# A fused attention and gated feed-forward kernel: new prices, new waits and new due times in the plan that sets the order of its instructions

## The chip, the cores and the metric

The kernel runs on one core of a Trainium2 chip. A core has several engines, each with its own in-order queue: TensorE (PE in the profile; its weight loads are shown apart as PEld), VectorE (DVE), ScalarE (ACT), GpSimd (POOL), and SyncE (SP), which here issues all DMA transfers. Engines wait for each other by semaphores. The metric is the device time of one execution in microseconds, the median of several runs.

## The reference

Eight batches of eight-head attention over 576 positions with head size 64, then a two-layer feed-forward with a gate. Cut to what matters:

```python
scores = np.matmul(q, k.transpose(0, 1, 3, 2)) / np.sqrt(D)        # (8, 8, 576, 576)
scores = np.where(block_i >= block_j, scores, -1e9)                # blocks of 64 positions
attn = np.exp(scores - scores.max(-1, keepdims=True))
attn = attn / (attn.sum(-1, keepdims=True) + 1e-9)
x = (attn @ v).transpose(0, 2, 1, 3).reshape(4608, 512)
h = x @ w_in                                                       # (512, 2048)
g = h * np.tanh(np.log1p(np.exp(np.minimum(h, 20))))               # mish
out = g @ w_out                                                    # (2048, 512)
```

All inputs and the output are float32.

## The kernel before

**Precision.** TensorE's large products use float16. Each operand is scaled by a power of two and split into a high half (a cast) and a low half (the remainder), and a product is the sum of three: high by high, high by low, low by high. The split is made by a cast on ScalarE, VectorE or GpSimd, and a subtraction on VectorE (`p_hi`, `p_lo`, lines 1088 to 1106, for the exponentials; `xh`, `xl`, lines 834 to 849, for queries and keys; `xt_hi`, `xt_lo`, lines 1211 to 1221, for the attention's output; `Gt`, lines 1350 to 1365, for the gated values). The heads of batch 0 alone are computed by float32 products (lines 954 and 1125), since nothing is split yet when the kernel begins.

**Attention.** A batch's 576 query positions are cut into two halves of 384 and 192. For each pair of heads (`load_pair`), each head and each half (`attend`), the work is a chain:
- first pass of scores on TensorE into a PSUM buffer `ss` (line 940, or 954 for batch 0); there are two such buffers;
- the maximum over key blocks, by copies (line 1003, ScalarE or VectorE) and `tensor_max` on VectorE (line 1016) into `mt`; these read PSUM;
- the maximum over partitions on GpSimd, `partition_all_reduce` into `mr` (line 1045);
- the negated maximum written into a row of `QB` (line 1052 on VectorE or 1059 on ScalarE);
- a second pass of scores that adds this row (line 940);
- the exponential on ScalarE (line 1070), a masking memset on GpSimd (line 1081), the split into `p_hi` and `p_lo`;
- the value products into the PSUM buffer `u` (line 1125), the sums and the division (lines 1172 to 1198), the split into `xt_hi` and `xt_lo`.

**Feed-forward.** Each half batch is a `Tile`, 16 in all. `turn` transposes its rows by DMA into `x_hi` and `x_lo` (line 1259). `m1` makes the products with `w_in` (line 1292) in four groups of 512 of the 2048 hidden columns and applies mish on ScalarE (line 1318) into `Et`, which has five slots, one for a group. `split` makes `Gt` from `Et`. `m2` makes the products with `w_out` (line 1394), scales them (line 1426 or 1433) and stores them.

**Shared space.** `Et` also holds batch 0's queries, keys and values in float32 until its heads are done, laid out pair by pair over the five slots. `Gt` holds pieces of `w_out` while the weights are read as 64-bit words and put together by integer operations on VectorE (lines 538 and 555), so the first `split` waits for all of `w_out`.

**The order.** No order is written by hand. Every step is an operation in a `Plan`: an engine with a price in microseconds, or several engines that could do it; the operations that it waits for; buffers taken and freed. `Plan.go` (line 164) plays the plan through engine by engine, taking at each engine the ready operation with the earliest due time. `Plan.order` (line 257) does so from the due times in the table `DUE`, passed back along the waits, then six times more backward and forward again, and keeps the shortest. The instructions are then emitted in the order of their planned starts, which fixes each engine's queue and which engine does a step that several could do. On the chip, semaphores wait for the true ends; the plan's times only set the order. The prices are small functions, which before read:

```python
def products(ns, full=False, rows=128):        # line 292; full: float32
    if full:
        return sum(n / 600 + 0.004 for n in ns), sum(n * rows / 32 for n in ns)

def pool(n):                                   # line 307
    return 0.42 + n / 300

def elem(n):                                   # line 311, casts on GpSimd
    return 0.2 + n / 780
```

The plan also models TensorE's clock (`pe_end`, line 239), table loads on ScalarE and transfers in flight.

Of the kernel before, what the change touches and what calls it, by code (L numbers as in the profile page):

```python
# [30 lines left out]
    "w": ((-17, 129.5, 276.5, 98), (186, 152, 293, 88)),  # L31
    "batch": (104, 216.5, 449.5, 454.5, 299.5, 543.5, 719.5, 647.5),
    "load": (
        (154.5, 254, 279, 266.5),
        (60, -40.5, 297, -132),
        (207.5, 299, 178.5, 157),
        (187, 199, 325, 217),
        (290, 323.5, 527.5, 588.5),
        (306.5, 436.5, 792, 494),
        (453.5, 894, 760.5, 651),  # L40
        (594.5, 471, 795.5, 666),
        (765, 662.5, 663.5, 727),
    ),
    "tile": (
        (-30.5, 39, -33.5, 25.5, 197.5, 303.5, 50, 51.5,
         254.5, 136.5, 239, 372, 191.5, 89, 162,
         278.5, 250.5, 219, 277.5, 192, 294.5, 190.5),
        (185.5, 251.5, -2.5, 309.5, 130.5, 233, -1, 73,
         102.5, 121.5, 148, 239, 158, -40.5, 279,
         358, 211.5, 275, 339, -89, 270.5, 268),  # L50
        (118.5, 386, 335.5, 400.5, 461.5, 282.5, 238, 182.5,
         418, 308.5, 219.5, 365, 379.5, -73.5, 297,
         314, 287.5, 305, 304, 380.5, 466.5, 271),
        (136, 112.5, 125, 241, 322.5, 144, 214, 393.5,
         459, 297, 395, 376, 444, -0.5, 291.5,
         307, 543, 524.5, 351, 337.5, 467.5, 195),
        (231, 326, 363, 300.5, 551.5, 477.5, 275.5, 335,
         336, 367.5, 368.5, 557, 415, -15, 587,
         624, 374, 360.5, 403, 630.5, 404, 785),
        (409.5, 381, 272.5, 532, 541.5, 549.5, 302, 496,  # L60
         404.5, 325, 449, 612.5, 457.5, 15, 441.5,
         417.5, 463, 526, 710, 290, 513.5, 304),
        (466.5, 602.5, 497.5, 373, 362.5, 311, 337, 301.5,
         502.5, 405.5, 522, 569, 411, 47, 512,
         576.5, 661, 564.5, 887.5, 719, 623.5, 582.5),
        (553, 697.5, 813.5, 516, 599, 519, 436, 516,
         568.5, 437.5, 558, 485.5, 428.5, -113.5, 511,
         568.5, 440.5, 560, 489, 239.5, 875, -158.5),
        (645, 444.5, 500.5, 908, 610, 755, 634, 470,
         563.5, 715.5, 637.5, 708, 506.5, 167.5, 666.5,  # L70
         677.5, 493.5, 637.5, 649.5, 675.5, 683, 743.5),
        (642.5, 302.5, 430, 330.5, 630.5, 547, 641.5, 619.5,
         890.5, 818.5, 558, 788, 609.5, -67.5, 753,
         610.5, 580.5, 585.5, 786.5, 53.5, 706.5, -90.5),
        (761.5, 414, 489.5, 582.5, 650, 594, 584.5, 847.5,
         865.5, 706, 756, 691, 832, -6, 825,
         700, 1028, 1041, 847, 955, 765.5, 735.5),
        (544, 643.5, 740, 539.5, 935, 669, 658, 939.5,
         799.5, 606, 745, 610, 742.5, -24.5, 878,
         698.5, 830, 882, 1243.5, 37, 892, 174),  # L80
        (804.5, 803.5, 895.5, 622, 731.5, 688.5, 716.5, 688,
         841, 726, 1131, 858, 1085, 161.5, 746.5,
         739.5, 705, 704, 923.5, 1136.5, 995.5, 777),
        (775, 681.5, 1052, 986, 790, 1115.5, 902.5, 1146,
         1028, 1017, 997.5, 1056, 1086, 98, 890,
         1003, 764.5, 1045.5, 892.5, -29.5, 962, 41.5),
        (971, 622.5, 587.5, 994.5, 1051, 814, 711, 1039,
# [35 lines left out]
class Plan:  # L123
# [16 lines left out]
    def __init__(self):  # L140
        self.ops = []

        self.slack = 0.0
# [1415 lines left out]
```

## Time and profile before

| | us |
|---|---|
| median of 3 runs (lowest, highest) | 1068.46 (1068.0, 1071.4) |
| profiled execution | 1066.92 |
| its span, first to last instruction | 1065.1 |
| PE busy in the span | 1002.3 (94%) |
| VectorE busy | 687.3 (65%) |
| ScalarE busy | 689.7 (65%) |
| GpSimd busy | 362.0 (34%) |

The granted TensorE clock has a mean of 0.97. In the profile's rows an operation reads: line, engine, operation, output tile <- input tiles, shape, count, busy time, mean time of one in ns, idle time of its engine before it and what ended it. In a timeline a row reads: start, duration, engine, line, operation, and in brackets the idle time before it with its releaser. In the rows of stretches each engine has its busy time and number of instructions; the last three numbers are the granted TensorE clock, the busy share of the DMA engines and GB/s. In rows of waits stand who waited, for whom, total us, how often, and the longest.

### The profile page before, as it was taken

The page shows a single profiled execution, that of the slowest core. Times are in us where ns is not written, and L with a number is a line of the kernel's source. Part 1 is how long each engine was busy: PE and PEld are TensorE (multiplying, and loading weights), DVE is VectorE, ACT ScalarE, POOL GpSimd, SP SyncE. Part 2 cuts the span into 40 slices and gives each one's busy share as a digit, 9 for nine tenths or more (in the row PEclk, how much of TensorE's full clock was granted, in tenths as well). Part 3 has the DMA queues.
Part 4 walks back from the last instruction along what each step waited for, and adds up shares of the span by engine and source line. Part 5 has one row for each costly group of instructions (what it writes and reads, how often), then busy time and mean ns, then how long its engine had stood idle before and what let it go on. Part 6 is the DMA issues. An engine that isn't in the chain of part 4 may idle for free. (4 is left out here: it accounts for less than half of the span.)

```text
span 1065.1 us, 25078 instructions
## 1 busy us (share of the span) xinstructions
PE 1002.3 (94%) x10016; PEld 759.3 (71%) x10016; DVE 687.3 (65%) x1520; ACT 689.7 (65%) x1047; POOL 362.0 (34%) x466
## 2 busy tenths in 40 slices
PE   4886989999999999989999999999999999999998
PEld 3564767686577777757777677876686677777777
DVE  5877799886678789777675886577771247212510
ACT  3556798658677899758875786687782466333531
POOL 3424245352544445353542642445520004000200
PEclk7668999999999999999999999999999999999999
DMA  9563432455134414443433342413441201200010
GB/s 321 185 186 100 130 101 76 117 124 145 41 109 114 126 45 129 102 116 89 124 79 80 100 127 71 118 51 89 116 87 38 59 23 44 53 9 9 16 31 24
DMA packets 118711, 98.65 MB, mean 93 GB/s; under 512 B 48449, under 2 KB 104769, under 8 KB 118593
## 3 DMA queue, kind: packets, MB, share of 16 engines
q1 hardware_dynamic: 118592, 97.04, 33.5%
q8 instruction: 79, 1.29, 0.5%
q14 instruction: 40, 0.32, 0.1%
HBM read 53.35 MB, written 9.44 MB: 59 GB/s over the span
## 5 line engine op out<-in xcount | busy, mean ns | idle before, releaser
L1394 PE MATMUL acc<-Gt,wo_h 128*128 128x192 f16 (+1 forms) x2048 | 393.2, 287 | 0.8 <-DVE ot L1426 0.8
L1045 POOL PARTITION_ALL_REDUCE mr<-mt x128 | 205.5, 1624 | 306.6 <-DVE mt L1016 290.6
L1292 PE MATMUL acc<-x_hi,wi_h 128*128 128x192 f16 (+1 forms) x1024 | 294.7, 288 | 2.3 <-ACT Et L1318 1.6
L1292 PE MATMUL acc<-x_hi,wi_l 128*128 128x192 f16 (+1 forms) x1024 | 294.6, 288 | 0.0
L1292 PE MATMUL acc<-x_lo,wi_h 128*128 128x192 f16 (+1 forms) x1024 | 294.6, 288 | 0.0
L1394 PE MATMUL acc<-Gt,wo_l 128*128 128x192 f16 (+1 forms) x1024 | 293.6, 287 | 0.0
L1292 PEld LDWEIGHTS <-wi_h 128*128 128x128 f16 x2048 | 190.0, 98 | 61.9 <-issue 7.1
L1394 PEld LDWEIGHTS <-wo_h 128*128 128x128 f16 x2048 | 190.2, 98 | 61.1 <-issue 2.1
L1318 ACT ACTIVATE Et<-acc,bv 128x384 f32<-128x384 f32 x192 | 110.0, 579 | 92.7 <-PE acc L1292 91.4
L1365 DVE SCALAR_TENSOR_TENSOR Gt<-Et,bv,Gt 128x1536 f16<-128x1536 f32 (+1 forms) x64 | 92.5, 1446 | 86.5 <-ACT Gt L1350 85.9
L1016 DVE TENSOR_TENSOR mt<-mt,ss 128x192 f32<-128x192 f32 (+3 forms) x448 | 121.5, 297 | 33.9 <-ACT mt L1003 29.4
L1106 DVE TENSOR_TENSOR p_lo<-pe,p_hi 128x896 f16<-128x896 f32 (+1 forms) x112 | 118.4, 1060 | 16.2 <-ACT p_hi L1088 11.3
L1292 PEld LDWEIGHTS <-wi_l 128*128 128x128 f16 x1024 | 100.5, 98 | 34.2 <-issue 1.5
L1394 PEld LDWEIGHTS <-wo_l 128*128 128x128 f16 x1024 | 100.3, 98 | 33.4 <-issue 0.3
L1070 ACT ACTIVATE pe<-ss,pv 128x896 f32<-128x896 f32 (+1 forms) x112 | 104.8, 953 | 21.2 <-DVE p_lo L1106 10.0
L1081 POOL MEMSET pe<- 64x64 f32 (+1 forms) x192 | 34.0, 207 | 221.6 <-ACT pe L1070 214.9
L940 PE MATMUL ss<-QB,KB 65*128 65x192 f16 (+7 forms) x512 | 68.2, 256 | 34.3 <-ACT QB L1059 22.9
L1125 PEld LDWEIGHTS <-p_hi 128*128 128x128 f16 x1680 | 86.8, 97 | 13.1 <-DVE tt L1198 2.7
L1125 PE MATMUL u<-V,p_hi 128*128 128x65 f16 (+1 forms) x1680 | 91.7, 193 | 3.1 <-DVE tt L1198 3.0
L1070 ACT ACT_TABLE_LOAD x66 | 84.7, 1283 | 14.6 <-PE ss L940 5.1
L1125 PE MATMUL u<-V,p_lo 128*128 128x65 f16 x840 | 87.3, 193 | 0.7 <-DVE p_lo L1106 0.7
L1318 ACT ACT_TABLE_LOAD x67 | 86.0, 1283 | 1.2
(105 smaller groups left out, 1205.6 us busy)
## 6 DMA issues: line engine op xcount, KB each, us to landing
QK<-xh SPq DMA_DIRECT2D x168, 72.0 KB, 2.1
out_dram<-ot SPq DMA_DIRECT2D x48, 192.0 KB, 2.0
wo_l<-in_w_in_dram SPq DMA_DIRECT2D x8, 1024.0 KB, 6.5
Gt<-in_w_out_dram SPq DMA_DIRECT2D x16, 512.0 KB, 4.2
ql<-in_q_dram SPq DMA_DIRECT2D x28, 288.0 KB, 3.2
kl<-in_k_dram SPq DMA_DIRECT2D x28, 288.0 KB, 3.2
VL<-in_v_dram SPq DMA_DIRECT2D x28, 288.0 KB, 3.1
VL<-in_v_dram SPq DMA_DIRECT2D x28, 256.0 KB, 3.2
```

The source lines that it names most:

```text
L940: nc.tensor.matmul(ss[:, col : col + q1 - qs], lhsT=k_[:, a, c * P : (c + 1) * P], rhs=q_[:, a, qs:q1], start=x == 0 and col % 512 == 0, s ...
L1016: nc.vector.tensor_max(t, t, sv(ss_[A.slot % NSS]))
L1045: lambda: nc.gpsimd.partition_all_reduce(mr[rm][:, 0:n], mx[:, 0:n], P, RED.max),
L1070: lambda: nc.scalar.activation(*spread(pe[rm], ss_[A.slot % NSS]), AF.Exp, scale=st.get("esc", D ** -0.5)),
L1081: nc.gpsimd.memset(t.rearrange("p (x y) -> p x y", x=k)[:, :, 0:64], 0.0)
L1106: lambda: nc.vector.tensor_sub(p_lo[rm][:, 0:W], pe[rm][:, 0:W], p_hi[rm][:, 0:W]),
L1125: nc.tensor.matmul(o, lhsT=l, rhs=r, start=start, stop=stop, skip_group_check=True)
L1292: nc.tensor.matmul(pt, lhsT=w[:, d, f * P : (f + 1) * P], rhs=x[:, d, :], start=k == 0 and d == 0 and z == 0, stop=d == NP - 1 and z == 2, ...
L1318: nc.scalar.activation(Et[:, (self.i * NG + g) % NE, j : j + K, 0:n], acc_[c.slot % NACC][:, 0 : K * n].rearrange("p (k n) -> p k n", k=K) ...
L1365: lambda g_hi=g_hi, g_lo=g_lo, ev=ev: nc.vector.scalar_tensor_tensor(out=g_lo, in0=ev, scalar=self.s_g, in1=g_hi, op0=ALU.mult, op1=ALU.su ...
L1394: nc.tensor.matmul(pt, lhsT=w[:, f, o * P : (o + 1) * P], rhs=g, start=k == 0 and f == 0 and z == 0, stop=f == NF - 1 and z == 2, skip_gro ...
```

## The change

Five things change, all of them in the plan; the computation stays.

- **VectorE holds GpSimd.** Operations that touch PSUM get the mark `psum=True`. While a VectorE operation without this mark runs, a GpSimd operation is planned to lose 0.82 of the overlap (`SHARE`), whichever begins first; its planned end is moved on accordingly. VectorE's own times aren't changed by GpSimd.
- **Prices.** A float32 product of at most 65 columns costs 0.226 us instead of n/600 + 0.004; a reduction on GpSimd costs 0.345 + n/356 instead of 0.42 + n/300.
- **Waits in `Et`.** The first five groups of `m1` and their mish wait for the heads of batch 0 whose inputs lie under their slot. The plan had no such wait before.
- **Tile 1 apart from tile 0.** The first `m1` product and the first mish of tile 1 (batch 0's second half) no longer wait for the last of tile 0, so that the groups of the two halves may alternate.
- **Due times.** All of `DUE` is replaced.

```diff
 DUE = {
-    "w": ((-17, 129.5, 276.5, 98), (186, 152, 293, 88)),
+    "w": ((384, 371.5, 301, 306.5), (72.5, 455, 389.5, 417.5)),
...
+    SHARE = 0.82
...
+                if done == 1 and end[i] > now:
+                    heapq.heappush(events, (end[i], 1, i))
+                    continue
...
+                if e == "dve" and not back and not ops[i].psum:
+                    locked = until[e]
+                    if until["pool"] > now:
+                        until["pool"] += self.lost(until["pool"] - now, us)
+                        end[pooled] = until["pool"]
+                if e == "pool" and not back:
+                    until[e] += self.lost(us, locked - now)
+                    pooled = i
...
+    def lost(self, us, lock):
+
+        return min(us / (1 - self.SHARE), max(lock, 0.0)) * self.SHARE
...
     if full:
-        return sum(n / 600 + 0.004 for n in ns), sum(n * rows / 32 for n in ns)
+        us = sum(n / 600 + 0.004 if n > 65 else 0.226 for n in ns)
+        return us, sum(n * rows / 32 for n in ns)
...
 def pool(n):
-    return 0.42 + n / 300
+    return 0.345 + n / 356
...
-                old.append(tiles[k // NG].splits[k % NG] if k >= 0 else [])
+                if k >= 0:
+                    old.append(tiles[k // NG].splits[k % NG])
+                    continue
+
+                w0 = (k + NE) * FG * Q0
+                old.append([
+                    x
+                    for p in range(NP)
+                    if p * FW < w0 + FG * Q0 and w0 < (p + 1) * FW
+                    for x in own[p]["ends"]
+                ])
...
                         if f == 0 and begin:
-                            after = after + [last.get("m1")]
+                            if self.i != 1:
+                                after = after + [last.get("m1")]
...
+                before = last.get("mish") if self.i != 1 else None
...
-                        [chain, self.batch["fc1"][g], last.get("mish")] + old[g],
+                        [chain, self.batch["fc1"][g], before] + old[g],
```

The mark `psum=True` is given to the copies and `tensor_max` of the maxima (lines 1003 and 1016), the sums and the division (lines 1172 to 1198) and the scaling of the outputs (line 1426).

More of the change, by code (lines that the diff above doesn't have):

```diff
@@ L149, in part, with add @@
             self.due = self.due[i]
-    def add(self, eng, us, emit, after=(), take=(), free=(), other=(), table=None):
+    def add(self, eng, us, emit, after=(), take=(), free=(), other=(), table=None, psum=False):
         self.ops.append(Op(eng, us, emit, after, take, free, self.due, other))
+        self.ops[-1].psum = psum
         self.ops[-1].table = table
@@ L1201, in attend @@
         o = add(
[L1202 removed]
+            "dve",
+            0.2 + dve(nqc * P, True),
+            weigh,
+            [sm],
+            free=[(u_ring, st["u", half][0])],
+            psum=True,
         )
```

124 lines of the change are left out of this document (63 added, 61 removed).

## The prediction

> **What bounds the kernel now.** I read the page's first part, then stretches of the span, then what the matmul engine waited for, then the places of the longest waits in order of time.
>
> ```profile
> span 1065.1 us, 25078 instructions
> PE 1002.3 (94%) x10016; PEld 759.3 (71%) x10016; DVE 687.3 (65%) x1520; ACT 689.7 (65%) x1047; POOL 362.0 (34%) x466
> ```
>
> ```profile
> core 0: us, PE busy (x) PEld busy (x) DVE busy (x) ACT busy (x) POOL busy (x), PEclk, DMA share, GB/s
> 0.00:100.00 100.00, 70.26 (x361) 49.53 (x362) 70.45 (x166) 50.58 (x90) 36.42 (x54) 0.73 0.66 205
> 150.00:800.00 650.00, 624.81 (x6889) 480.77 (x6888) 495.22 (x1118) 490.64 (x756) 284.85 (x355) 0.99 0.38 98
> 800.00:1065.10 265.10, 259.68 (x2406) 196.08 (x2404) 78.85 (x140) 106.31 (x149) 24.16 (x35) 1.00 0.11 30
> ```
>
> TensorE (PE) sets the time. The edit removes no matmul, so it can move only PE's idle time and slow clock. Idle is 1065.1 − 1002.3 = 62.8 us: 29.7 in the first 100 us, 25.2 between 150 and 800, 5.4 after that. In the first 100 us the granted clock is 0.73, so its 70.26 us of work would take about 51 at full clock: another 19 us, as an estimate. Some 80 us in all can move.
>
> PE's waits in the first 100 us, then from 100 to 850:
>
> ```profile
> PE ss L940 <- ACT QB L1059: 15.1, 3, 8.3
> PE ss L940 <- DVE QB L1052: 6.6, 4, 2.8
> ```
>
> ```profile
> PE ss L940 <- ACT QB L1059: 7.8, 5, 2.6
> PE ss L940 <- ACT pe L1070: 7.7, 12, 1.8
> PE ss L940 <- DVE QB L1052: 4.5, 7, 1.4
> ...
> PE acc L1292 <- ACT Et L1318: 1.6, 2, 1.4
> ```
>
> Most of it is the second pass of scores (L940) waiting for the negated maxima in QB, which wait for GpSimd's reduction over partitions (mr, L1045). Its longest case, from the timelines of five engines and two stretches:
>
> ```profile
> 79.70 3.48 DVE L555 SCALAR_TENSOR_TENSOR wo_h<-wo_l,wo_h 128x1024 int32<-128x1024 int32 x3
> ...
> 83.78 2.48 DVE L555 SCALAR_TENSOR_TENSOR Gt<-Gt 128x512 int32<-128x512 int32 x4
> ```
>
> ```profile
> 60.37 0.41 POOL L574 PARTITION_ALL_REDUCE wv<-wv  x1 [2.00 <-ACT wi_h L566]
> ...
> 80.84 5.74 POOL L697 PARTITION_ALL_REDUCE bv<-bv  x1 [5.98 <-ACT VL L690]
> ```
>
> ```profile
> 77.72 1.26 SPq L1259 DMA_TRANSPOSE x_lo<-xt_lo  x1
> ```
>
> ```profile
> x_lo<-xt_lo SPq DMA_TRANSPOSE x40, 2.5
> ```
>
> ```profile
> 87.88 0.85 PE L940 MATMUL ss<-QB,KB 1*128 1x192 f16 x5 [8.26 <-ACT QB L1059]
> 88.66 0.50 PE L1292 MATMUL acc<-x_hi,wi_h 128*128 128x384 f16 x1
> ```
>
> ```profile
> 80.00:90.00 10.00, 2.12 (x10) 0.97 (x10) 6.26 (x9) 2.55 (x7) 7.62 (x4) 0.65 0.54 163
> 90.00:100.00 10.00, 10.00 (x75) 7.46 (x74) 7.33 (x25) 7.92 (x10) 1.04 (x4) 0.84 0.19 49
> ```
>
> A reduction of four columns, done elsewhere in 0.41 us, lasts 5.74 while VectorE runs seven two-input integer operations for w_out, which nothing needs yet. The maxima's reduction is queued behind it on GpSimd, QB behind that, and PE stands 8.26 us. The products of w_in (L1292) stand behind the waiting L940 in PE's queue, though their last input was sent at 77.72 and takes 2.5 to land: ready at 80.2, begun at 88.66. Afterwards the clock is 0.84 for 10 us, 1.6 us more.
>
> **The change part by part.** Hardly an instruction is added or removed (copies and casts may change engine); the order is made anew by a plan with other prices, waits and due times. So the cost lies in which waits of PE go and which come.
>
> *(a) VectorE holding GpSimd, at the stop above.* A plan that charges 0.82 of the overlap sees the 5.3 us (5.74 − 0.41) that the old plan could not, and can put the integer work or the reduction of bv elsewhere. Bounds: 0, and 8.26 + 1.6 = 9.9 gained. I take 5, about the middle, because the products brought forward meet the new waits of (d).
>
> *(b) The other early reductions.*
>
> ```profile
> 9.72 2.83 POOL L1045 PARTITION_ALL_REDUCE mr<-mt  x2 [7.32 <-DVE mt L1016]
> ...
> 37.12 4.65 POOL L1045 PARTITION_ALL_REDUCE mr<-mt  x2 [6.51 <-DVE mt L1016]
> ...
> 50.92 5.03 POOL L1045 PARTITION_ALL_REDUCE mr<-mt  x2 [1.47 <-DVE mt L1016]
> ```
>
> ```profile
> 41.30 0.48 PE L940 MATMUL ss<-QB,KB 1*128 1x256 f16 x3 [0.51 <-DVE QB L1052]
> ...
> 54.58 0.79 PE L940 MATMUL ss<-QB,KB 1*128 1x256 f16 x3 [2.48 <-ACT QB L1059]
> ```
>
> A pair takes 2.83 us undisturbed, 1.8 and 2.2 more in the two later cases; PE then waits 0.51 and 2.48. Bounds 0 and 3.0 gained; I take 2, nearest to the second row.
>
> *(c) The same after 100 us, with all other consequences of a new order.*
>
> ```profile
> L1045 POOL PARTITION_ALL_REDUCE mr<-mt x128 | 205.5, 1624 | 306.6 <-DVE mt L1016 290.6 <-DVE dv L1197 8.6 <-DVE dv L1179 3.2
> ```
>
> ```profile
> L1045 POOL PARTITION_ALL_REDUCE mr<-mt x128: 876/1424/5717, 9.7 to 1002.0; - x128
> ```
>
> Half of the 128 reductions have 384 columns (1.42 us, half of the pair at 9.72) and half 192 (0.88, the minimum). Undisturbed they would take 64 × 1.42 + 64 × 0.88 = 147 us, so 58 of the 205.5 is stretch: 0.45 us each. PE waits for QB twelve times after 100 us, 12.3 us in all; 12 × 0.45 = 5.4 goes if the stretch goes. Upper bound 12.3. Downward, a new order can bring new waits: I bound that by a third of the 25.2 us idle, 8 lost. I take 5 gained. The cheaper base price of the reduction (0.345 + n/356: 1.42 and 0.88) agrees with these rows, and its effect is in here. So is the price of the float32 value products:
>
> ```profile
> 39.34 1.45 PE L1125 MATMUL u<-Et,pe 128*128 128x65 f32 x12
> ```
>
> Each product is two records, so 1.45/6 = 0.24 us against 0.112 in the old plan and 0.226 in the new. That is right, and only moves planned times: bounds 0 and 2 gained, I take 0.
>
> *(d) New waits for the space in Et.* Batch 0's queries, keys and values lie in Et, and the plan now knows that a group of w_in products may start only when the heads of the pairs under its slot are done, in both halves.
>
> ```profile
> 77.40 2.22 PE L1125 MATMUL u<-Et,pe 128*128 128x65 f32 x18
> ...
> 95.16 4.23 PE L1125 MATMUL u<-Et,pe 128*128 128x65 f32 x36
> ...
> 105.64 0.33 PE L1292 MATMUL acc<-x_hi,wi_h 128*128 128x384 f16 x1
> 105.81 0.33 PE L1292 MATMUL acc<-x_lo,wi_h 128*128 128x384 f16 x1
> ```
>
> Group 0 needs pair 0, whose last values end at 79.6: no wait. Group 1 (from 105.64 today) needs pair 1, which ends at 99.4. In today's order the wait is already met, and costs 0. If group 0 starts at 80.2, its 48 products at 0.17 (the step between the last two rows) take 8.2 us and the heads' work in between about 8 (4.23 of it the values at 95.16; the rest, scores, is estimated), so PE runs dry near 97 and stands up to 3 us until 99.4 and the division behind it. I take 1 lost; bounds 0 and 3.
>
> *(e) Alternation of the halves.* Tile 1's group 0 has Et's fifth slot; its groups 1 to 3 need slots that tile 0 frees by its split, which waits for the whole of w_out, by code.
>
> ```profile
> 147.60 0.25 PE L1292 MATMUL acc<-x_hi,wi_h 128*128 128x192 f16 x1
> ```
>
> So only 48 products of 192 columns (some 4 us of PE) can come ahead, as a filler where PE has little to fill: it waited 1.6 us for Et. Bounds 0 and 1.6 gained; I take 0.
>
> *Sum.* 5 + 2 + 5 − 1 + 0 = 11 us. The profiled execution took 1066.9 us (span 1065.1); 1066.9 − 11 = 1055.9. The runs' median, 1068.5, is 1.5 above the profiled one, so I predict **1057** for the median.
>
> **A rule against it.** The plan charges every VectorE operation outside PSUM, and only GpSimd loses. Two rows say otherwise:
>
> ```profile
> 761.86 1.50 POOL L1045 PARTITION_ALL_REDUCE mr<-mt  x1
> ```
>
> ```profile
> 762.00 0.79 DVE L461 TENSOR_SCALAR pv<-pv 128x2 int32<-128x2 int32 x1 [0.31 <-POOL pv L813]
> ...
> 650.96 0.16 DVE L461 TENSOR_SCALAR pv<-pv 128x2 int32<-128x2 int32 x1
> ```
>
> A single-input operation of two columns, 0.16 us elsewhere, takes 0.79 beside a reduction that is hardly stretched (1.50 against 1.42). There GpSimd held VectorE. The Trainium skill, "SBUF — State Buffer", section "SBUF: two separate sides", calls the shared port pair an exclusive lock: whichever starts first has it for its whole instruction, VectorE holding it in a two-port mode or with two SBUF inputs. These rows agree that it goes both ways; the 0.82 charge is one-sided.
>
> **The rivals.** *Stretch moved, not removed* (no difference). If GpSimd starts first more often, VectorE's operations become late by 0.6 us each (0.79 − 0.16), and the maxima, which VectorE makes, start late. For: the rows just shown. Against: at 80.84 GpSimd clearly lost. Then (c) is 0, (a) and (b) are partly spent on it; some 1066 on the median.
>
> *The first 100 us shrink as a whole* (larger gain). Of 29.7 us idle and 19 of slow clock there, 22 instead of 6 go, because a PE with fewer stops also keeps its clock: 1066.9 − 22 − 5 = 1040, median 1041. For: clock and idle sit together (0.65 at 80 to 90). Against: batch 0's eight steps of scores, maximum, exponential and values follow each other whatever the order.
>
> *GpSimd overpriced* (slower). The charge also falls on the casts of the exponentials:
>
> ```profile
> L1099 POOL CAST p_hi<-pe x59: 824/1026/2807, 139.3 to 1003.3; 128x768 f16<-128x768 f32 x32, 128x896 f16<-128x896 f32 x27
> ```
>
> The unchanged price for 768 columns, 0.2 + 768/780 = 1.18, lies above the traced minimum 0.82 already; with 0.82 of every overlap on top, GpSimd looks occupied when it isn't, and the plan casts elsewhere. If half of the 59 go to ScalarE or VectorE at about 1.03 us, they put 30 us on engines that have 159 and 155 of 650 idle. If a third of it falls ahead of a maximum or an exponential on which PE waits, PE loses 10 us between 150 and 800, and (a) to (c) don't come since the early order is mispriced too: 1066.9 + 10 = 1077, median 1078. It decides once about 30 casts have moved; with 10 it costs 3 and the gain stands. Against: a cast can also go to an engine that is free.
>
> **How the numbers follow.** Forecast (1050 to 1064) 0.50; whole first stage 0.12; stretch moved 0.14; overpriced GpSimd 0.24. What a measurement can tell from no change is 0.3%, 3.2 us. Faster is the first two, 0.62; within 0.3% the third, 0.14; slower 0.24. The range runs from the second case's 1041 to the fourth's 1078: below it lies the deeper half of the second (0.06), above it under half of the fourth (0.10). It takes in the sum's bounds: all gains at most, 9.9 + 3.0 + 12.3 + 2 + 1.6 = 29, give 1040; losses at most, 8 + 3, give 1079.
>
> **What would show it.** (a): no reduction near 5 us in the first 100 us and no wait of PE over 4 us. (b), (c): L1045's mean below 1.5 us and PE's waits for QB clearly under 34. (d): PE idle near 97 to 100 while w_in products stand ready. (e): 192-column products of L1292 before the 384-column ones are done, without shorter idle. Overpricing: far fewer than 59 casts by GpSimd. The prediction is wrong if PE's idle stays at 63 us or more, or if the time falls although L1045 stays at 1.6 us.

## The result and the profile after

The changed kernel takes **1036.14 us** (median of 4 runs, 1033.62 to 1036.75), beside 1069.38 for the kernel before on the same chip (4 runs, 1068.0 to 1071.4): a ratio of 0.9683, 95% interval 0.9659 to 0.9707, some 33 us. That is faster, and 21 us below the forecast of 1057; it lies below the range too, which ended at 1041. The profiled execution took 1036.75 us, with a span of 1034.9 (before: 1066.92 and 1065.1).

The page's first part for the kernel after, with the span and the busy time of each engine:

```profile
span 1034.9 us, 25108 instructions
PE 999.5 (97%) x10016; PEld 762.4 (74%) x10016; DVE 705.7 (68%) x1583; ACT 706.5 (68%) x1033; POOL 336.1 (32%) x443
```

PE's busy time fell by 2.8 us (1002.3 to 999.5), its idle time by 27.4 (62.8 to 35.4). Nearly all of the gain is idle time. The view of stretches says where it went; its columns are those of the same view before, from which the row of 100 to 150 us is added here:

```profile
100.00:150.00 50.00, 47.55 (x368) 32.97 (x366) 42.74 (x98) 42.15 (x54) 16.58 (x23) 0.97 0.45 125
```

After:

```profile
core 0: us, PE busy (x) PEld busy (x) DVE busy (x) ACT busy (x) POOL busy (x), PEclk, DMA share, GB/s
0.00:100.00 100.00, 76.64 (x351) 53.57 (x351) 81.69 (x197) 62.07 (x100) 31.52 (x54) 0.78 0.76 234
100.00:150.00 50.00, 49.38 (x408) 36.38 (x407) 45.82 (x101) 40.42 (x52) 20.29 (x21) 1.00 0.30 90
150.00:800.00 650.00, 643.46 (x7036) 494.72 (x7035) 499.61 (x1141) 496.63 (x733) 255.12 (x328) 1.00 0.37 96
800.00:1034.90 234.90, 230.07 (x2229) 177.70 (x2227) 78.60 (x146) 107.33 (x150) 29.17 (x41) 1.00 0.13 35
```

| PE idle, us | 0 to 100 | 100 to 150 | 150 to 800 | 800 to the end |
|---|---|---|---|---|
| before | 29.7 | 2.45 | 25.2 | 5.4 |
| after | 23.4 | 0.6 | 6.5 | 4.8 |

Each entry is the length of a stretch less PE's busy time in it. The long steady stage gave up 18.7 us, the first 100 us only 6.3.

The longest stop before was 8.26 us. What PE waited for in the first 100 us of the kernel after (who waited, for whom, total us, times, longest):

```profile
PE ss L960 <- ACT QB L1080: 13.4, 6, 4.4
PE ss L974 <- DMA Et<-in_k_dram: 4.6, 1, 4.6
PE ss L960 <- DVE QB L1073: 4.6, 4, 3.1
```

Lines are numbered anew: L960 is the second pass of scores (L940 before), L974 the float32 scores of batch 0 (L954), L1080 and L1073 write QB (L1059 and L1052), L1066 is the reduction (L1045), L1091 the exponential (L1070), L1146 the value products (L1125), L1220 the division's output `tt` (L1198), L1329 the products with `w_in` (L1292). The waits for QB fell from 21.7 to 18.0 us there.

The same in the steady stage, 150 to 800 us, first before, then after:

```profile
PE ss L940 <- ACT QB L1059: 7.8, 5, 2.6
PE ss L940 <- ACT pe L1070: 6.7, 11, 1.8
PE ss L940 <- DVE QB L1052: 4.5, 7, 1.4
PE u L1125 <- DVE tt L1198: 2.8, 6, 1.0
```

```profile
PE ss L960 <- ACT pe L1091: 2.0, 3, 1.2
PE acc L1329 <- DMA x_lo<-xt_lo: 1.2, 2, 0.7
PE ss L960 <- DVE QB L1073: 0.9, 2, 0.6
PE u L1146 <- DVE tt L1220: 0.9, 2, 0.5
```

The waits for QB are all but gone (12.3 to 0.9 us), and those for the exponential and the division fell with them (9.5 to 2.9). Yet the reduction itself hardly got faster. Its group, over the whole kernel after (count, busy us, mean ns of one, GpSimd's idle time before it):

```profile
L1066 POOL PARTITION_ALL_REDUCE mr<-mt x128 | 212.6, 1674 | 298.1 <-DVE mt L1037 278.7 <-DVE dv L1219 5.5 <-DVE bv L748 3.7
```

The mean was 1624 ns before; now it is 1674. In the steady stage alone it went from 1682 to 1652 (97 and 96 reductions). **The stretch, that is, what a reduction takes beyond its undisturbed time, stayed, and PE no longer waits for it.** One case of each kernel shows how. Before, from the timeline near 400 us (start, duration, and in brackets the idle time before it and its releaser):

```profile
399.88 1.79 POOL L1045 PARTITION_ALL_REDUCE mr<-mt  x1 [1.36 <-DVE mt L1016]
399.97 0.94 DVE L1106 TENSOR_TENSOR p_lo<-pe,p_hi 128x768 f16<-128x768 f32 x1
...
401.70 0.25 DVE L1052 TENSOR_SCALAR QB<-mr 1x192 f16<-1x192 f32 x1 [0.65 <-POOL mr L1045]
...
402.00 0.52 PE L940 MATMUL ss<-QB,KB 65*128 65x192 f16 x5 [0.33 <-DVE QB L1052]
```

A reduction of 192 columns (0.88 us undisturbed) begins together with a two-input subtraction of 0.94 us and takes 1.79: the overlap is lost nearly whole. The second pass comes 2.12 us after the reduction's start, and PE stands 0.33. After, near 305 us:

```profile
304.87 0.80 DVE L869 SCALAR_TENSOR_TENSOR xl<-kl,pv,xh 128x576 f16<-128x576 f32 x1
...
305.11 3.57 POOL L1066 PARTITION_ALL_REDUCE mr<-mt  x1 [0.68 <-DVE mt L1037]
...
305.60 0.80 DVE L869 SCALAR_TENSOR_TENSOR xl<-ql,pv,xh 128x576 f16<-128x576 f32 x1
...
306.85 0.54 DVE L1248 TENSOR_TENSOR xt_lo<-tt,xt_hi 128x384 f16<-128x384 f32 x1
...
307.62 1.28 DVE L1405 SCALAR_TENSOR_TENSOR Gt<-Et,bv,Gt 128x768 f16<-128x768 f32 x1
...
309.23 0.52 ACT L1080 ACTIVATE QB<-mr 1x384 f16<-1x384 f32 x1
...
311.46 0.49 PE L960 MATMUL ss<-QB,KB 65*128 65x256 f16 x3
```

A reduction of 384 columns (1.42 us undisturbed) is stretched to 3.57 beside four operations with two inputs and one with a single input (0.60 us from 306.32). PE doesn't wait: the second pass stands in its queue where it begins 6.35 us after the reduction's start, 1.7 after QB is written (309.75), and `w_in` and `w_out` products fill the time. Over the 97 reductions of the steady stage before and 96 after, the median time from the reduction's start to its second pass went from about 3.45 to about 4.15 us, and the share of second passes that begin less than 0.5 us after their QB is written from 31% to 10%.

### The profile page after: what moved, and what is told of

Read it like the earlier page. It is cut to its first block, busy times and chain, and to the rows that moved or that the text cites. A ratio compares the mean times of both kernels' runs of the same rounds, so it can differ in the third digit from the quotient of the medians.

```text
span 1034.9 us, 25108 instructions
## 1 busy us (share of the span) xinstructions
PE 999.5 (97%) x10016; PEld 762.4 (74%) x10016; DVE 705.7 (68%) x1583; ACT 706.5 (68%) x1033; POOL 336.1 (32%) x443
## 4 chain that ended last, share of the span: by engine, by line
PE 70%; DVE 11%; ACT 6%; issue 3%; DMA 3%; SPq 3%; POOL 2%; ACTq 0%; DVEq 0%; POOLq 0%
PE acc L1434 29%; PE acc L1329 27%; PE u L1146 7%; PE ss L960 6%; SPq L1286 2%; DVE mt L1037 2%; ACT pe L1091 2%; POOL mr L1066 2%; ACT L1091 1%; PE ss L974 1%; DMA QB<-xl 1%; DVE p_lo L1127 1%; DVE Gt L1405 1%; DVE xl L869 1%; SPq L888 1%
## 5 line engine op out<-in xcount | busy, mean ns | idle before, releaser
L1066 POOL PARTITION_ALL_REDUCE mr<-mt x128 | 212.6, 1674 | 298.1 <-DVE mt L1037 278.7
L1329 PE MATMUL acc<-x_lo,wi_h 128*128 128x192 f16 (+1 forms) x1024 | 294.1, 287 | 1.2 <-DMA x_lo<-xt_lo 1.2
L1329 PE MATMUL acc<-x_hi,wi_h 128*128 128x192 f16 (+1 forms) x1024 | 294.2, 287 | 0.2
L1329 PE MATMUL acc<-x_hi,wi_l 128*128 128x192 f16 (+1 forms) x1024 | 294.1, 287 | 0.0
L1329 PEld LDWEIGHTS <-wi_h 128*128 128x128 f16 x2048 | 189.3, 98 | 56.4 <-issue 4.1
L1037 DVE TENSOR_TENSOR mt<-mt,ss 128x192 f32<-128x192 f32 (+3 forms) x448 | 123.8, 298 | 26.0 <-ACT mt L1023 21.5
L1127 DVE TENSOR_TENSOR p_lo<-pe,p_hi 128x896 f16<-128x896 f32 (+1 forms) x112 | 116.4, 1040 | 21.1 <-ACT p_hi L1109 19.9
L1329 PEld LDWEIGHTS <-wi_l 128*128 128x128 f16 x1024 | 100.4, 98 | 34.5 <-issue 2.0
L1091 ACT ACTIVATE pe<-ss,pv 128x896 f32<-128x896 f32 (+1 forms) x112 | 106.2, 954 | 23.0 <-PE ss L960 13.5
L1146 PEld LDWEIGHTS <-p_hi 128*128 128x128 f16 x1680 | 87.1, 97 | 11.3 <-issue 1.3
L1146 PE MATMUL u<-V,p_hi 128*128 128x65 f16 (+1 forms) x1680 | 91.2, 193 | 1.1 <-DVE tt L1220 0.9
L1146 PE MATMUL u<-V,p_lo 128*128 128x65 f16 x840 | 87.3, 193 | 0.3 <-DVE p_lo L1127 0.3
L960 PE MATMUL ss<-QB,KB 65*128 65x192 f16 (+7 forms) x512 | 67.6, 255 | 19.0 <-ACT QB L1080 13.4
```

The costliest lines, as they stand in the source:

```text
L960: nc.tensor.matmul(ss[:, col : col + q1 - qs], lhsT=k_[:, a, c * P : (c + 1) * P], rhs=q_[:, a, qs:q1], start=x == 0 and col % 512 == 0, s ...
L1037: nc.vector.tensor_max(t, t, sv(ss_[A.slot % NSS]))
L1066: lambda: nc.gpsimd.partition_all_reduce(mr[rm][:, 0:n], mx[:, 0:n], P, RED.max),
L1091: lambda: nc.scalar.activation(*spread(pe[rm], ss_[A.slot % NSS]), AF.Exp, scale=st.get("esc", D ** -0.5)),
L1127: lambda: nc.vector.tensor_sub(p_lo[rm][:, 0:W], pe[rm][:, 0:W], p_hi[rm][:, 0:W]),
L1146: nc.tensor.matmul(o, lhsT=l, rhs=r, start=start, stop=stop, skip_group_check=True)
```

## The experiments

By the *hold* is meant what the plan now charges: that a VectorE operation keeps GpSimd from going on. Theory A: knowing the hold, the plan puts more other products ahead of the second pass, and this, not the due times, empties the steady stage of idle time. Theory B: the new due times are just a better table. Further rivals are named where they are tried. PE's idle time in us for every version, worked out as above from one profiled execution each, beside the ratio to the kernel before with its 95% interval:

| kernel | ratio | 0 to 100 | 100 to 150 | 150 to 800 |
|---|---|---|---|---|
| before | 1 | 29.7 | 2.45 | 25.2 |
| after | 0.9683 [0.9659, 0.9707] | 23.4 | 0.6 | 6.5 |
| e1_new_due_old_prices | 0.9929 [0.9904, 0.9955] | 21.6 | 6.6 | 19.2 |
| e2_old_due_new_plan | 0.9868 [0.9842, 0.9893] | 40.0 | 5.9 | 4.0 |
| e3_no_hold | 0.9925 [0.9902, 0.9948] | 23.0 | 4.4 | 19.5 |
| e4_chained | 0.9735 [0.9703, 0.9766] | 24.6 | 0.2 | 8.3 |
| e5_flat, e5b_flat | 0.9771 [0.975, 0.9793] | 26.8 | 3.4 | 8.2 |
| e6_two_input | 0.9692 [0.9674, 0.971] | 24.75 | 1.9 | 7.2 |
| e7_one_stop | 1.0007 [0.999, 1.0024] | 22.25 | 2.45 | 25.4 |
| e8_old_value_price | 0.9881 [0.9854, 0.9908] | 28.2 | 2.2 | 11.7 |
| e9_early_due | 0.9766 [0.975, 0.9783] | 25.6 | 0.2 | 13.1 |
| e10_search_hold | 0.9706 [0.969, 0.9722] | 28.0 | 1.0 | 5.9 |
| e11_search_no_hold | 0.9978 [0.9962, 0.9993] | 25.4 | 1.8 | 24.9 |
| e12_search_old_value | 0.9822 [0.9788, 0.9856] | 32.0 | 0.35 | 5.7 |
| e13_fill | 0.9704 [0.9674, 0.9734] | 19.4 | 0.6 | 5.0 |
| e14_two_search | 0.9673 [0.9645, 0.9701] | 21.1 | 2.35 | 6.15 |

Three of these versions, e1, e2 and e8, give a wrong output: it is off by 0.10 in relative error, all of it in batch 0's first half. The code says why. `scores_own` (line 969 after) looks up its two score buffers in `st["rooms"]` only when it is emitted, and by then the entry of the second half has replaced that of the first. This does no harm while the plan hands out the two buffers in the same order in both halves. In these three orders it doesn't for two of the four pairs, and the two heads of such a pair get each other's weights. Instructions and shapes are the same either way, and both heads' scores are one operation of the plan, so their times are kept as evidence. What has to stand without them rests on e3, e5, e10, e11 and e12, whose output is right.

### The new due times alone, the new plan alone

The kernel after with the old prices and no hold (e1), with no hold alone (e3), and with all of the new plan but the old table of due times (e2):

```diff
-    SHARE = 0.82
+    SHARE = 0.0
...
-        us = sum(n / 600 + 0.004 if n > 65 else 0.226 for n in ns)
+        us = sum(n / 600 + 0.004 for n in ns)
...
-    return 0.345 + n / 356
+    return 0.42 + n / 300
```

> The changed kernel with all prices of before (VectorE's hold not charged, float32 value products at n/600 + 0.004, reductions at 0.42 + n/300); the new due times, the waits in Et and the freed halves stay. Theory A, the gain comes from the prices (an order made with false prices runs into waits on the chip): 1058 to 1075 us, PE idle about 55 to 65 us of which 20 or more between 150 and 800. Theory B, the gain comes from the new due times whatever the prices: 1036 to 1046 us, idle between 150 and 800 under 12.

```diff
-    SHARE = 0.82
+    SHARE = 0.0
```

> The changed kernel with VectorE's hold on GpSimd not charged (SHARE 0 instead of 0.82), all else kept, the cheaper reduction too. Theory A with the hold as the price that matters: 1055 to 1070 us, waits of PE for QB after 100 us back above 8. Theory A with another price, or theory B: 1036 to 1046.

```diff
-    "w": ((384, 371.5, 301, 306.5), (72.5, 455, 389.5, 417.5)),
+    "w": ((-17, 129.5, 276.5, 98), (186, 152, 293, 88)),
...
```

> The changed kernel with the due times of before; prices, waits and freed halves are the new ones. Theory A: due times not searched for these prices give a longer plan, but one that the chip keeps to: 1055 to 1068 us, with idle between 150 and 800 below the 25 of before, and PE's waits for QB after 100 us below 6. Theory B: as before the change, 1066 to 1080, idle between 150 and 800 at 25 or more.

Measured: e1 1060.73 us (1059.42 to 1062.56), e3 1060.75 (1058.68 to 1061.7), e2 1054.44 (1052.66 to 1055.49). Without the charge for the hold the steady stage keeps most of its idle time, whichever due times there are. With it and the old due times it is as empty as it gets. From the view of stretches, e3 and e2:

```profile
150.00:800.00 650.00, 630.54 (x6843) 482.80 (x6840) 489.85 (x1102) 497.91 (x715) 248.91 (x334) 0.99 0.35 93
```

```profile
0.00:100.00 100.00, 59.99 (x269) 43.34 (x270) 87.74 (x195) 54.87 (x95) 32.59 (x51) 0.74 0.76 244
100.00:150.00 50.00, 44.13 (x319) 34.16 (x319) 39.57 (x94) 29.41 (x41) 15.61 (x19) 0.86 0.24 69
150.00:800.00 650.00, 645.98 (x7179) 500.37 (x7176) 508.21 (x1172) 515.48 (x762) 251.73 (x340) 1.00 0.37 98
```

Theory A holds for the steady stage. e2 loses in its first 150 us, where PE idles 46 us in place of 24: due times found for other prices fit the beginning badly. The parts don't add up either: the new due times without the charge bring 8 or 9 us (e1, e3), the new plan with the old due times 15, both together 33.

### The same search for each set of prices

e2 and e1 mix a table with prices that it wasn't found for. So three versions got due times of their own, by one search: from the table of before, changed for 40 minutes, each change kept that shortens the length that the plan itself works out when the kernel is built. e10 has the whole new plan, e11 no hold and the old price of a reduction, e12 the whole new plan but the old price of a float32 value product.

e11, beside its own `DUE`, then e12:

```diff
-    SHARE = 0.82
+    SHARE = 0.0
...
-    return 0.345 + n / 356
+    return 0.42 + n / 300
```

```diff
-        us = sum(n / 600 + 0.004 if n > 65 else 0.226 for n in ns)
+        us = sum(n / 600 + 0.004 for n in ns)
```

> The changed kernel's plan with due times found by a search of my own: 40 minutes of random changes from the due times of before, keeping those that shorten the plan. Same search as the next run. Theory A (an order made with the hold charged is kept by the chip): idle of PE between 150 and 800 under 10 us, 1038 to 1050 us. Theory B (only these particular due times are good): 1055 or more.

> The same search, begun from the same due times and for the same time, with the plan that doesn't charge the hold and has the reduction's price of before; float32 value products at the new price, waits in Et and freed halves kept. Its plan came out 13 us shorter than that of the run before. Theory A: the chip doesn't keep to it, idle between 150 and 800 15 us or more, 1052 to 1072 us, slower than the run before by 8 or more. Theory B: as fast as the run before or faster.

> The changed kernel with the float32 value products at their price of before (0.112 us), the hold charged, and due times from the same 40 minutes' search begun from the due times of before. If that price matters by itself: PE idle in the first 150 us above 33 (29 in e10_search_hold) and 1046 to 1060 us. If only the due times of e8 were unfit: 1034 to 1046, within 8 us of e10_search_hold's 1038.

Measured: e10 1038.23 us (1035.7 to 1038.94), e11 1066.54 (1064.17 to 1070.15), e12 1051.09 (1049.61 to 1052.58). e11's plan was the shortest of the three, 1012.2 against e10's 1025.6, and on the chip it took 28 us longer. What PE waited for between 150 and 800 us, e11 and then e10, where line numbers are 27 lower than in the kernel after:

```profile
PE ss L933 <- ACT QB L1053: 9.1, 10, 2.3
PE ss L933 <- ACT pe L1064: 4.9, 10, 1.1
PE u L1119 <- DVE tt L1193: 4.8, 6, 2.1
PE acc L1302 <- ACT Et L1331: 3.1, 3, 2.5
```

```profile
PE u L1119 <- DVE p_lo L1100: 1.9, 1, 1.9
PE ss L933 <- ACT pe L1064: 1.6, 7, 0.3
PE acc L1302 <- DMA x_lo<-xt_lo: 0.9, 2, 0.5
PE u L1119 <- DVE tt L1193: 0.8, 2, 0.6
PE ss L933 <- DVE QB L1046: 0.2, 1, 0.2
```

With the hold left out, the waits of every step behind the reduction are there, for QB, the exponential, the division and the mish; with it they shrink together. And both have reductions stretched alike (means of 1684 ns in e11, 1648 in e10). e11 also has the old base price of a reduction, but that makes its reductions dearer in the plan, not cheaper. Theory B falls: with equal search, what is charged decides. Each search was made once, so how much of the 28 us is the luck of a search isn't known; that e3, with other due times, loses 25 us says that it isn't most. The share of second passes that begin less than 0.5 us after their QB is written, worked out as above, is 16 to 31% in the four versions without a charge (before, e1, e3, e11) and 4 to 15% in all that charge the hold. The span exceeds the plan's own length by 44 to 64 us where the hold isn't charged (before 64, e1 44, e3 46, e11 52) and by 5 to 29 where it is (e2 5, e10 10, after 18, e12 29).

e12 loses 13 us although its steady stage is as full as e10's. The stretch 0 to 150 us, e12 and e10:

```profile
0.00:150.00 150.00, 117.62 (x591) 84.80 (x591) 108.54 (x264) 87.12 (x137) 42.46 (x70) 0.78 0.59 183
```

```profile
0.00:150.00 150.00, 120.97 (x723) 85.53 (x723) 127.78 (x296) 96.09 (x147) 50.71 (x76) 0.87 0.59 187
```

PE is busy for about as long, but runs 591 instead of 723 instructions, at a granted clock of 0.78 instead of 0.87: a plan that prices batch 0's value products at half their time gets less done at the beginning. The clock differs in every execution: its mean over the span is 0.958 to 0.972 in e12's four and 0.979 to 0.982 in e10's. Why the order of e12 gets the lower clock is not shown.

### The old price of float32 value products, due times as after

```diff
-        us = sum(n / 600 + 0.004 if n > 65 else 0.226 for n in ns)
+        us = sum(n / 600 + 0.004 for n in ns)
```

> The changed kernel with the float32 value products at their price of before (0.112 instead of 0.226 us); the hold stays charged. If this price carries the gain of the first 150 us: PE idle there 33 us or more (24 after the change, 32 before), and 1045 to 1060 us. If it is worth nothing by itself, as predicted: idle between 150 and 800 as after the change (under 10) and 1034 to 1048.

Measured: 1055.07 us (1052.75 to 1058.75), 19 more than after, with due times that weren't found for it; e12 gives 13 with due times of its own. Of e8's 12 us of added idle time, 6 are in the first 150 us and 5 in the steady stage. e1 and e3 differ in this price too (and in the reduction's base price) and are equal, so with these due times it is worth something only where the hold is charged as well.

### The halves in a chain again

```diff
-                            if self.i != 1:
+                            if True:
                                 after = after + [last.get("m1")]
...
-                before = last.get("mish") if self.i != 1 else None
+                before = last.get("mish")
```

> The changed kernel with tile 1's first w_in product and first mish waiting for tile 0's last again; all else kept. If the alternation of the halves is worth nothing by itself, as predicted: 1033 to 1042 us (a few us by the chance of another order). If it carries the gain of the first 150 us: 1043 to 1050, with the loss before 200 us.

Measured: 1039.42 us (1037.77 to 1043.56), 3.3 more than after; the intervals of the ratios touch ([0.9703, 0.9766] and [0.9659, 0.9707]). The alternation is worth 3 us at most.

### A flat surcharge in place of the hold

```diff
-    SHARE = 0.82
+    SHARE = 0.0
...
-    return 0.345 + n / 356
+    return 0.345 + n / 356 + 0.8 * (n >= 192)
```

> The changed kernel with the hold not charged, but every reduction of the maxima priced 0.8 us dearer, a flat sum above the mean stretch of 0.45. Theory A1, the plan must know which VectorE operation holds which reduction: idle of PE between 150 and 800 at 15 or more, 1050 to 1062 us. Theory A2, the price only has to make the plan leave the maxima more time, so that other products stand ahead of the second pass of scores: idle there under 10, 1036 to 1050 us.

> The kernel with the flat price of reductions again (0.8 us dearer, hold not charged), for its profile. Theory A1: idle between 150 and 800 at 15 us or more. Theory A2: under 10.

Measured: 1043.5 us for e5_flat, the median of three executions (1042.48 to 1044.92); a fourth, the profiled one, took 2067 and is left out, so the profile is that of e5b_flat, the same kernel (1044.55 us, span 1042.8). From its view of stretches:

```profile
150.00:800.00 650.00, 641.81 (x6985) 493.51 (x6984) 487.19 (x1123) 517.77 (x736) 242.99 (x334) 1.00 0.37 95
```

PE's idle time in the steady stage is 8.2 us. So most of the gain there needs no knowledge of who holds whom: every reduction is planned 0.8 us longer, and something else is put ahead of its second pass. Charging the operations that do hold brings another 7 us, most of it in the first 150 us (30.2 us idle against 24.0).

### Only two-input operations hold

```diff
+        names = {"scalar_tensor_tensor", "tensor_sub"}
+        self.ops[-1].two = not psum and bool(names & set(emit.__code__.co_names))
...
-                if e == "dve" and not back and not ops[i].psum:
+                if e == "dve" and not back and ops[i].two:
```

> The changed kernel in which only VectorE operations with two SBUF inputs (the subtractions and scalar_tensor_tensor) hold GpSimd; operations with one input are not charged, as the trace before the change showed. If the over-charge costs something, GpSimd gets more casts than 48 and the idle between 150 and 800 falls under 6.5 us; if it is only slack, the idle there is 4 to 10 and the time 1034 to 1050, moved by the first 150 us alone.

Measured: 1035.44 us (1034.14 to 1035.83), no different from after; the casts `p_hi` by GpSimd are 49, after 48. Whether operations with one input are charged too doesn't matter. This version with due times sought for 50 minutes from those of after:

> The changed kernel in which only VectorE operations with two inputs in SBUF are planned to hold GpSimd, and whose due times were sought again for 50 minutes from those of after, each change kept that shortens the plan's own length (1022.5 with the due times of after, 1014.0 with these; after's own plan is 1017.1 long). If the chip now follows the plan wherever the hold is charged (the span lay 10.6 above the plan's length in the two-input version and 18 in after), the span is 1025 to 1032, the median 1026 to 1034 and PE's idle time between 150 and 800 us stays at 4 to 9 us. If the rest of the gap is made of waits that the plan prices wrongly, shortening the plan by 3 to 8 us buys nothing: 1034 to 1042, with more idle in the first 150 us than after's 24.

Measured: **1032.63 us** (5 runs, 1031.23 to 1033.23), the fastest of all; its ratio to before, 0.9673 [0.9645, 0.9701], can't be told from after's. The span, 1030.1, is 16 above the plan's length, against 10.6 in e6: of the 8.5 us by which the search shortened this version's plan, the span got 3 (1033.1 to 1030.1). What is left is at the beginning: 23.4 of its 33.6 us of idle time lie in the first 150 us.

### One stop taken out by hand

The kernel before, its order changed at the stop near 80 us alone: the pair of maxima's reductions goes first, then the reduction of `bv`, then the integer operations, and the two writes of QB behind the maxima go to VectorE.

```diff
     ops = plan.order()
+    one = {o.i: o for o in ops}
+    for i in (251, 262):
+        one[i].eng = "dve"
+        one[i].us, one[i].emit = one[i].ways["dve"]
+    late = [one[i] for i in (251, 262, 672, 85, 82, 86, 351, 355, 352, 356, 353, 357)]
+    ops = [o for o in ops if o not in late]
+    at = ops.index(one[261]) + 1
+    ops[at:at] = late
```

> The kernel before, with one stop mended by hand: near 80 us the two reductions of the maxima go ahead of the reduction of bv on GpSimd, their QB rows are written by VectorE, and the seven two-input integer operations come behind these on VectorE; nothing else moves. Step (a) of the prediction: PE's wait of 8.26 us falls to under 3, and 4 to 6 us of it arrive at the end, 1062 to 1065 against 1069. If the loss is covered elsewhere anyway, 1067 to 1070.

Measured: 1069.45 us (12 runs), ratio 1.0007 [0.999, 1.0024]: nothing gained. The stop is gone, as the timeline of e7 shows, where the pair of maxima's reductions takes 1.79 us and that of `bv` 0.53:

```profile
80.34 1.79 POOL L1045 PARTITION_ALL_REDUCE mr<-mt  x2 [5.15 <-DVE mt L1016]
...
81.88 0.53 PE L940 MATMUL ss<-QB,KB 1*128 1x192 f16 x5 [1.67 <-DVE QB L1052]
...
82.04 0.53 POOL L697 PARTITION_ALL_REDUCE bv<-bv  x1
...
91.11 7.94 PE L1125 MATMUL u<-Et,pe 128*128 128x65 f32 x36 [0.48 <-DVE bv L701]
```

PE waits 1.67 instead of 8.26 us, and the second pass begins 6.0 us earlier (81.88 against 87.88). In this execution the clock then takes it back. From the view of stretches of e7:

```profile
80.00:90.00 10.00, 6.66 (x42) 3.67 (x42) 8.41 (x17) 5.00 (x8) 3.76 (x6) 0.83 0.24 69
90.00:100.00 10.00, 9.52 (x46) 8.65 (x44) 8.36 (x25) 5.44 (x7) 0.40 (x1) 0.52 0.46 142
```

In the kernel before, PE was busy 12.1 us in these 20 with 85 instructions; in e7 it is busy 16.2 us with 88. The group of value products (36 records) that took 4.23 us begins 4.05 us sooner and takes 7.94 at a granted clock of 0.52: it ends at 99.05, before at 99.39. The lead is gone. That nothing is gained is the median of twelve executions; that the clock is the reason is read from one profile of each kernel. The clock also differs between these two where the order is the same (0.57 before and 1.00 in e7 from 10 to 20 us), so chance may have a part in it.

### New due times for the beginning alone

The kernel after with its own due times for the weights, batches 0 and 1, the first two rows of `load` and the first three tiles, the old ones for the rest:

```diff
-    "batch": (43, 232, 700, 449.5, 217.5, 549.5, 932, 565.5),
+    "batch": (43, 232, 449.5, 454.5, 299.5, 543.5, 719.5, 647.5),
...
```

> The changed kernel with the new due times only for the weights, batches 0 and 1, the loads of batch 0 and 1 and the first three tiles; all later ones are those of before. If the new due times work mainly in the first 150 us: PE idle there 22 to 32 us (24 after the change, 46 with the due times of before), 1034 to 1046. If the gain of the due times is spread over the run: 1046 to 1056.

Measured: 1044.7 us (1043.29 to 1047.0). The first 150 us are as after (25.7 us idle, after 24.0; e2: 46), so the new due times do there what e2 lacked. But the steady stage idles 13.1 us, more than with either whole table under the new plan (e2 4.0, after 6.5): a table works as one piece.

### Keeping the clock up

In the kernel after, the granted clock is 0.67, 0.50, 0.50 and 0.62 in the four stretches of 10 us from 60 to 100. Here the kernel after keeps its own order, and 57 fills (two products of 224 columns of zeros each, into a free accumulator; work added, nothing left out) stand ahead of six of batch 0's second passes.

```diff
+    FILL = {0: 14, 5: 5, 7: 2, 8: 12, 9: 14, 10: 10}
...
+        if getattr(o, "own", False):
+            slot = next(s for s in range(NACC) if s not in live.values())
+            emits += [lambda slot=slot: fill(slot)] * FILL.get(seen, 0)
```

> The changed kernel in its own order, with 57 short products of zeros (2 times 224 columns each, into a free accumulator that nobody reads) put ahead of six second passes of batch 0's scores, where PE stood longest in the first 90 us. Theory: the clock is granted by how busy PE was; with the gaps filled it stays up, PE's 44 us at half clock in the first 100 us shrink to under 25, and the end comes 3 to 12 us earlier: 1024 to 1033. Rival: the chain of the heads sets the pace whatever the clock, or the filling delays the products behind it: 1034 to 1042.

Measured: 1038.44 us (1035.0 to 1040.69), no gain. The clock was higher where the fills stood (1.00, 0.83, 0.55 and 0.60 in the same stretches), but over the first 100 us it is 0.78 in both kernels, so the clock was moved rather than raised; and the second pass near 86 us came no earlier. PE's idle time in the table counts the fills as work. The timeline of e13 (line numbers 2 higher), then that of after:

```profile
79.86 0.43 DVE L560 TENSOR_SCALAR Gt<-Gt 128x512 int32<-128x512 int32 x1 [2.39 <-DMA Gt<-in_w_out_dram]
...
82.55 4.04 POOL L1068 PARTITION_ALL_REDUCE mr<-mt  x2 [8.90 <-DVE mt L1039]
...
86.33 0.84 PE L962 MATMUL ss<-QB,KB 1*128 1x192 f16 x5 [7.88 <-DVE QB L1075]
```

```profile
79.60 0.43 DVE L558 TENSOR_SCALAR Gt<-Gt 128x512 int32<-128x512 int32 x1 [0.72 <-DMA Gt<-in_w_out_dram]
...
82.29 4.03 POOL L1066 PARTITION_ALL_REDUCE mr<-mt  x2 [7.03 <-DVE mt L1037]
...
86.07 0.85 PE L960 MATMUL ss<-QB,KB 1*128 1x192 f16 x5 [3.14 <-DVE QB L1073]
```

PE got there 4.5 us sooner (78.45 against 82.93) and waited so much longer (7.88 against 3.14). VectorE stands at a piece of `w_out` that is still under way (2.39 and 0.72 us), with batch 0's maxima queued behind it, and the pair of reductions takes 4.0 us again. At this second pass the transfer, VectorE's order and GpSimd set the pace, not PE and its clock.

## Why the prediction was wrong in size

**What bounds the kernel** was read rightly: PE sets the end, the edit removed no product, and 27.4 of the 30.2 us by which the span fell are PE's idle time. The step that failed is (c), and in it the sentence "PE waits for QB twelve times after 100 us, 12.3 us in all; 12 × 0.45 = 5.4 goes if the stretch goes. Upper bound 12.3."

**(c)** has two errors. First, the mechanism: the stretch did not go (1624 to 1674 ns), so "12 × 0.45" prices something that didn't happen. What went is the plan's ignorance of it. The waits did not shrink by the stretch: the plan knows that QB comes later and puts other products ahead, and in the steady stage 11.4 of the 12.3 us went. Second, the bound: a delay of the reduction that the plan doesn't know also delays the exponential, its split, the values and the division. The waits for the exponential and the division stood in the same view (7.7 and 2.8 us between 100 and 850; the second is not among the rows shown in the prediction), and e10 and e11 show that they come and go with the charge. The row that bounded this term was the stage's whole idle time, 25.2 us, which the prediction used only to bound the loss. Measured: 18.7 gained in place of 5. With 25.2 for the bound in place of 12.3, all gains at most would have been 42, and the low end 1027.

**The float32 value price**, inside (c), "is right, and only moves planned times: bounds 0 and 2 gained, I take 0". e12 and e8 say 13 and 19 us where the hold is charged too. Planned times make the order, and the prediction names no work that would hide a wrong one. Batch 0's heads have 240 records of such products, so 120 products, and at 0.112 in place of 0.226 us the plan leaves out 13.7 us of PE (120 × 0.114), all of it at the beginning.

**(a)** had 5 of at most 9.9. By itself it is worth nothing (e7: ratio 1.0007 [0.999, 1.0024]). The prediction counted the slow clock after the stop as a further 1.6 us of gain; in e7's profiled execution PE begins 6 us sooner and its clock is 0.52 from 90 to 100 us, in place of 0.84. In the kernel after, the 8.26 us stop is a 3.14 us one, in a chain that a `w_out` transfer holds up.

**(a) and (b)** together, with (d), gave 6 for the first 100 us. PE's idle time fell by 6.3 there and by 1.8 in the 50 us behind. The size is near, and no reduction of the first 100 us is near 5 us any more: the longest pair, at 31.68, takes 4.23. But the pair ahead of the second pass at 86 us, of 192 columns each, still takes 4.03 us, against twice 0.88 undisturbed. What part of the new order brought the 6.3 us is not settled by these runs, so the nearness may be luck.

**(d)** is not seen: no row of PE's waits in the first 150 us is one for a mish or for a slot of Et, and the stretch from 90 to 100 us is full (PE busy 9.86 of 10 us). **(e)** was bounded by 1.6 us; e4 measured 3.3, within the uncertainty of the two ratios.

**The rivals.** *Stretch moved, not removed* was half right: the stretch stayed. Its conclusion, no gain, took the stretch for the cost. *The first 100 us shrink as a whole* had the nearest time, 1041, and the wrong place: they gave 6.3 of idle time, and the clock rose only from 0.73 to 0.78. *GpSimd overpriced* fell: of 59 casts 48 stayed with GpSimd, and charging fewer operations (e6) changed nothing. The prediction did name what would show it wrong, "if the time falls although L1045 stays at 1.6 us", and that is what happened.

**The rule against it** concerned the charge being one-sided. The Trainium skill, "SBUF — State Buffer", section "SBUF: two separate sides", calls the shared port pair an exclusive lock. The row at 399.88 agrees for a two-input subtraction (0.91 us lost beside 0.94). The case at 305.11 does not agree that the one that starts first has it for its whole instruction: GpSimd's reduction had begun, and yet the two-input operations from 305.60 and 306.85 took 0.80 and 0.54 us, as short as anywhere in this kernel. Only the one from 307.62 took longer, 1.28 in place of the 1.00 to 1.02 of the 31 others of its size. There VectorE lost some 0.26 us and GpSimd 2.15, so a charge on GpSimd alone comes near. For the time it made no difference which operations were charged (e6), as long as something was (e3, e5).

## What to carry to other kernels

Where an order is planned ahead, a delay costs most where the plan doesn't know of it; to price it can be worth as much as to remove it, since the plan covers what it sees. So bound the gain of a better price by all the waits of the stage that lie behind the mispriced step, not by the wait for that step. A plan's own length says nothing across different prices (e11's was shorter than e10's and ran 28 us longer), and time won back at one stop can be lost again before it reaches the end (e7). A buffer that is looked up only at emission must not be a name that later code sets anew: the order of a plan decides whether it shows.

## What the runs showed of the hardware beyond that

- A low clock can cost little or much, by what PE has to do in it: in the kernel before the granted clock is 0.65 from 80 to 90 us, when PE is busy 2.12 us, and 0.84 in the next 10; in e7 it is 0.83 and then 0.52, and 36 records of float32 value products take 7.94 us in place of 4.23.
- With fills PE is busy 8.56 instead of 3.48 us between 60 and 70 us and has a clock of 1.00 instead of 0.67 there, but over the first 100 us the clock is 0.78 in both, and where PE waits for other engines 20 us later it buys nothing.
- VectorE's two-input operations do not hold GpSimd quite for their whole length: in the case at 305.11 four of them overlap the reduction by 2.96 us (0.56, 0.80, 0.54 and 1.06), and it loses 2.15 (3.57 − 1.42), 0.73 of the overlap; the plan's 0.82 is near. The one-input operation beside it (0.60 us) would make the share smaller still.
